# Two attention steps and an MLP: p of batches 2 to 7 turned by a DMA transpose, six output buffers, last stores on two queues, a new order of the opening

## The chip, the cores and the metric

The kernel runs on one core of a Trainium2 chip. The metric is device time in microseconds; the median of three runs before the change is 248.39 us (248.11 to 248.7). A profiled execution gives the trace that is read here.

## The reference

Shapes: 8 batches, 8 heads, 576 tokens, head size 64, 32 packed tokens; then an MLP with width 512, hidden 2048. The inputs and the output are float32.

```python
def sm_attn(qq, kk, vv):
    s = scale * np.matmul(qq, kk.transpose(0, 1, 3, 2))
    s = s - np.max(s, axis=-1, keepdims=True)
    a = np.exp(s)
    a = a / (np.sum(a, axis=-1, keepdims=True) + 1e-09)
    return np.matmul(a, vv)
p_packed = sm_attn(p, k, v)             # 32 packed tokens look at all 576
out = sm_attn(q, p_packed, p_packed)    # all 576 look at the 32
# x: out with the heads side by side, 4608 x 512
h = x @ w_in
r = np.maximum(h, 0.0)
g = s * (r * r) + b                     # s and b are scalars
return g @ w_out
```

## The kernel before, in words

Everything is computed in bf16 with float32 sums. The second attention step and the first MLP product are folded: the packed result of a batch (ppd) is multiplied with w_in once (pw, "W" below), and the hidden tile is pw times the attention weights aT, so the attention output itself is never made. The scalar s is applied and b's share added when the output leaves: ysb = s * (g part) + biasrep, where biasrep is b times the column sums of w_out.

The work of one batch, by the letters of the kernel's own list of steps:

- L: loads, all issued from the POOL queue (line 124 and after), cast from float32 on the way. k, q and v arrive with 96 rows in the partitions. Lk, Lq, Lv load a batch; Lp, Lpall load p of batch 1 and of batches 2 to 7; Lwi, Lwo load parts of w_in and w_out; Lsb loads s and b. Each of k, q and v has one buffer, so the next batch's load waits for the last reader.
- D (line 261): k and q of batches 2 to 7 are turned by a DMA transpose issued from SP, straight into kT and qT (two buffers each). T (line 222, 248): k and q of batches 0 and 1 are turned on TensorE, 12 transposes a half, and copied out of PSUM by ACT or DVE.
- V (line 268): DVE brings v into the order that the products need.
- PD, PP, PA, PPA: p is written twice side by side, turned on TensorE and copied into pbd, from which the first scores take it. Batches 0 and 1 have their own (line 186); batches 2 to 7 are one tile, pall, 96 partitions with 16 x 128 elements, turned in 16 transposes (prep_pall, line 201) and brought into pbd by eight copies, four on DVE and four on ACT.
- F, P, X, S, A: first scores and exp (line 280), product with v and division (305), its transpose into ppd (332), second scores and exp (339), and the weights by a product with ones, a logarithm, an exp of its negative and a multiplication (434). F needs kT and pbd; S needs ppd and qT.
- W (449): pw in four groups of 512 columns. M (501): a hidden tile of 128 x 576 in four matmuls of 288 columns, then relu on ACT or DVE and the square on DVE into gT. O and Q (line 545): an output tile of 128 rows in 16 matmuls of 512 columns, summed in one PSUM bank; Q evacuates it on DVE into one of five ysb buffers and stores it in two pieces (store, line 534). The last tile of all is done in two halves of 256 columns.
- BT (515): column sums of w_out on TensorE, summed and scaled on DVE. Z (596): matmuls on zeros, whose result nobody reads; they stand between real work in the first 21 us.

Batch 0 is cut into smaller steps for the opening: W0 in eight groups of 256 columns, h (line 473) in place of M, and exp0, logs0, inverse0 (lines 385 to 407) for its two parts u and, before the change, for each set a by itself.

The order is a list of words written out by hand in the kernel's last part (run, line 638). Each engine and each queue takes its own instructions in the order of this list; a helper (line 73, and lines 62 and 65 for matmul and transpose) pins it. A word with "@" names PSUM banks and issues the matmuls; the same word again, with "a" or "v", issues the evacuation on ACT or DVE. Stores and DMA transposes share SP's queue, so that an instruction that waits there holds up all behind it. On DVE, before the change, the doubling of pall (PA) stands early, in the middle of batch 1's weights; the reorder of v of batch 2 comes 15 us later.

Of the kernel before, what the change touches and what calls it, by code (L numbers as in the profile page):

```python
# [14 lines left out]
def kernel(  # L15
# [41 lines left out]
    outp = ctx.enter_context(tc.tile_pool(name="outp", bufs=5))  # L57
# [47 lines left out]
    pall = constp.tile([16 * (B - 2), 16, 2, D], BF16, name="pall")  # L105
    identb = constp.tile([P, P], BF16, name="identb")
# [24 lines left out]
    def load_part(what, part):  # L131

        if what == "q":
            if part == 0:
                raw["q", 0] = rawp.tile([R, H, NC * D], BF16, tag="qn", name="qn")
            x = slice(PARTS[part][0] * P, PARTS[part][1] * P)
            pool.dma_start(
                out=raw["q", 0][:, :, x],
                in_=q[0].rearrange("h (r c) d -> r h (c d)", c=NC)[:, :, x],
            )  # L140
            return
        if part == 0:
            raw[what, 0] = rawp.tile([R, H, NC * D], BF16, tag=what + "n", name=what + "n")
        pool.dma_start(
            out=raw[what, 0][:, 4 * part:4 * part + 4, :],
            in_={"k": k, "v": v}[what][0].rearrange("(g a) (r c) d -> a r g (c d)", a=2, c=NC)[part],
        )
# [53 lines left out]
    def prep_pall():  # L201
        n = 16 * (B - 2)
        pts = [take(1, BF16)[:, 0] for _ in range(2)]
        for t in range(16):
            tr(
                pts[t // 8][:, (t % 8) * P:(t % 8) * P + n],
                pall[:, t, :, :],
                identb[0:n, 0:n],
            )
        for x in range(2):  # L210
            yield
            src = pts[x].rearrange("p (t n) -> p t n", n=P)[:, :, 0:n].rearrange(
                "p t (x a i) -> p a x i t", a=2, i=JJ
            )
            for c2 in range(2):
                for a in range(2):
                    out = pbd[D * c2:D * c2 + D, a, 2:B, :, c2, :].rearrange(
                        "p b g (i t) -> p (b g) i t", i=JJ
                    )[:, :, :, 8 * x:8 * x + 8]
                    (act.copy if x else vec.tensor_copy)(out=out, in_=src[D * c2:D * c2 + D, a])  # L220
# [164 lines left out]
    def exp0(u, a):  # L385
        w = part(u)[1]
        act.activation(
            out=cut(e2[0][:, a], u), in_=s2[u][:, :, a * w:(a + 1) * w], func=AF.Exp, scale=scale
        )
# [7 lines left out]
    def logs0(u, a):  # L397
        w = part(u)[1]
        if ("l", u) not in rcd:
            rcd["l", u] = smp.tile([P, 2, 2 * w], F32, tag="ld", name="ld")  # L400
            rcd["r", u] = smp.tile([P, 2, 2 * w], F32, tag="rcd", name="rcd")
        act.activation(out=rcd["l", u][:, a], in_=s2["d", u][:, a, 0:2 * w], func=AF.Ln)

    def inverse0(u, a):
        act.activation(out=rcd["r", u][:, a], in_=rcd["l", u][:, a], func=AF.Exp, scale=-1.0)
# [138 lines left out]
    class Out:  # L544
        def __init__(self, col, parts, cuts=(0, NB)):
            self.col, self.parts, self.m, self.cuts = col, parts, 0, cuts
            self.yps = self.ysb = None

# [17 lines left out]
        def leave(self):  # L566
# [8 lines left out]
            for b, col, n in self.parts:  # L575
                store(self.ysb, d0, d1, i0, b, col, n, act if d0 else sp)
# [8 lines left out]
    def outs(b):  # L585
        t0, g0 = tail(b), slot(b) * S
        c0 = 0 if t0 else TAIL
        res = [Out(g0 + c0 + t * P, [(b, c0 + t * P, P)]) for t in range(NT)]
        if b % 2:
# [3 lines left out]
            res.insert(0, Out(slot(both[0][0]) * S + both[0][1], both))  # L593
# [10 lines left out]
    def ops(what, n):  # L604
# [24 lines left out]
        else:  # L629
            return {  # L630
                "h": mlp_in0, "M": mlp_in, "Z": idle, "Lpall": load_pall, "Lwo": load_w_out, "Lsb": load_sb, "PP": prep_p,
                "PA": lambda: twice(pall), "PPA": lambda _: prep_pall(), "F": first_scores, "e": exp0, "d": sums0,
# [5 lines left out]
    def run(word):  # L638
# [9 lines left out]
        elif what == "Q":  # L648
            todo[n[0], n[1]].leave()
        elif word in begun:  # L650
# [19 lines left out]
    run("Lk0.1")  # L670
    run("Lv0.0")
    run("Lv0.1")
    run("Lq0.0")
# [10 lines left out]
    run("Z12@7")  # L684

    for word in """
        Lq0.1 PD0 PP0@1 Tk0.0@2 Tk0.0a Tk0.0a PP0a Z2@0 Tk0.1@4 Tk0.1a PP0v Lp1 Tk0.1v V0.0 Z2@6 F0.0@2
        F0.0 Z5@7 P0.0@0 P0.0 F0.1@4 F0.1 Lwi0.1 Z1@1 X0.0 X0.0v V0.1 Z4@1 P0.1 P0.1 Tq0.0@2 Tq0.0a
        Tq0.0v Z2@1 Tq0.1@1 Tq0.1v Tq0.1a X0.1 X0.1v S0.0.0@6 Lwi2.4 Z1@4 S0.0.1 e0.1 S0.1.0@2 S0.1.1
        Z3@5 d0.1@0 e0.0 d0.0 e1.1 e1.0 W0.0@4 d1.1@6 l0.0 PD1 W0.0v d1.0 l1.0 i1.0 G1.0 Z6@2 W0.3@2  # L690
        W0.3v W0.3v l0.1 W0.2@0 Lwi6.8 W0.2v Z6@2 W0.7@2 l1.1 W0.6@6 i1.1 G1.1 W0.2a PP1@0 Lwi1.2 i0.1
        G0.1 W0.0a i0.0 G0.0 W0.7a PP1v PP1a W0.7a h0.6.0@4 W0.6v W0.6a W0.1@0 W0.1a W0.1a h0.6.0v
        h0.12.1@2 h0.6.0 h0.12.1a h0.12.1 h0.4.1@6 h0.14.0@4 h0.4.1a h0.14.0a h0.0.1@0 h0.0.1v h0.0.1
        h0.14.1@2 h0.14.0 h0.4.1 h0.6.1@6 h0.4.0@4 h0.6.1a h0.6.1 h0.14.1a Lk1 Tk1.0@0 h0.4.0a Tk1.0v
        Tk1.0v h0.14.1 h0.2.1@6 h0.2.1a h0.12.0@2 Lwi4.6 Tk1.1@4 Tk1.1a h0.4.0 h0.2.0@0 W0.5@6 h0.12.0a
        Tk1.1v W0.4@4 W0.4a W0.4v h0.2.0a h0.2.1 h0.12.0 W0.5v F1.0@2 F1.0 h0.0.0@4 h0.0.0v W0.5a
        h0.8.0@0 h0.8.0a F1.1@2 h0.10.0@6 Lv1 V1 h0.8.0 F1.1 P1.1@4 h0.2.0 h0.10.0a h0.0.0 h0.8.1@0
        h0.8.1a h0.10.1@2 h0.10.1a Lq1 Tq1.0@6 Tq1.0a Tq1.0a P1.1 X1 X1v Tq1.1@0 Tq1.1v W1.0@2 W1.1@4
        Tq1.1v W1.0v W1.0a S1@6,0 S1 S1 W1.3@2 W1.3v W1.3v Lwo0.4 O0.2x2@6 O0.1x2@7 Lpall O0.2x2 h0.8.1
        A1.0@0 O0.0x3@2 W1.1a W1.1a A1.0 PA O0.0x1 A1.0 A1.0 O0.3x3@3 A1.1@4 A1.1 O0.1x1 Lwo4.8 PPA0@0,1  # L700
        Lsb O0.0x1 h0.10.1 O0.0x1 O0.2x1 O0.1x1 O0.3x1 Lwo8.12 A1.1 A1.1 O0.1x2 M1.4@4 O0.3x3 Lwo12.16
        PPA0 PPA0 O0.0x2 M1.4a M1.4 h0.10.0 O0.3x1 M1.2@4 O0.1x3 M1.2a M1.2 Lv2 W1.2@0 W1.2a BT@4 Lk2
        Lq2 O0.1x1 W1.2v M1.6@0 M1.6a O0.1x1 O0.0x1 O0.1x1 Dk2 O0.3x7 M1.3@0 O0.3x1 M1.3a BT M1.5@4
        O0.2x2 M1.1@0 M1.3 M1.5a M1.5 O0.2x3 M1.6 M1.1a M1.1 M1.8@4 M1.8a O0.2x2 M1.15@0 O0.2x1 M1.15a
        V2 O0.0x2 M1.15 M1.0@4 Dq2 PPA0 Q0.3 O0.0x2 M1.0a M1.0 M1.9@0 M1.9a M1.9 M1.14@4 M1.14a O0.0x3
        Q0.0 O0.2x3 M1.7@0 Lq3 Q0.2 F2.0@4 M1.7v M1.8 F2.1@2 O0.1x1 F2.0 M1.7 O0.1x3 M1.10@0 M1.14 F2.1
        P2.1@6 Lk3 M1.10a P2.1 M1.13@4 M1.13a M1.13 M1.12@2 M1.12a X2 M1.11@0 M1.11a X2v O1.4x2@4 Q0.1
        O1.4x2 PPA0 O1.0x1@5 W2.2@2 W2.2v W2.2v S2@0,6 S2 S2 M1.11 O1.0x2 O1.4x1 O1.0x2 M1.10 A2.0@0
        A2.0 A2.0 A2.1@2 O1.1x1@6 M1.12 O1.3x2@7 W2.0@0 W2.0v W2.0v O1.0x1 Lv3 O1.1x6 W2.3@0 A2.0 Dk3
        A2.1 A2.1 A2.1 W2.1@2 W2.3a W2.3a O1.4x1 O1.3x2 Lk4 O1.3x1 O1.4x2 M2.10@0 O1.1x1 O1.3x2 M2.10v  # L710
        O1.1x1 M2.10 O1.1x2 O1.0x2 O1.1x1 M2.0@0 W2.1v W2.1a O1.0x2 O1.1x1 M2.0v M2.0 V3 M2.5@2 M2.5a
# [82 lines left out]
```

## Time and profile before

| what | us |
|---|---|
| median of three runs | 248.39 |
| the profiled execution, in all | 247.68 |
| its span, first to last instruction | 245.9 |
| TensorE matmuls busy in the span | 237.0 |
| DVE, ACT, POOL busy | 163.8, 126.9, 30.6 |
| matmuls on zeros, first 21 us | 13.5 |
| granted TensorE clock, mean | 0.997 |

The difference of 1.8 us between the execution and its span lies around the program. In the lines of the profile "L62 PE MATMUL banks<-gT" reads: line 62 of the kernel, the engine, the operation, what is written and read. PE is TensorE, PEld its weight loads, SPq, ACTq and POOLq the queues of the engines that issue DMAs. A matmul's duration contains its pipeline; the time from one start to the next is shorter. In the view of 40 slices a digit is the busy share in tenths. In the chain view the work that ended last is followed back from the end, start and length first.

### The profile page before, as it was taken

The numbers are of one execution on the slowest core, as the hardware profiler recorded it, in microseconds if no ns is written. First come the engines' busy times: TensorE is split into PE (matmuls) and PEld (weight loads), VectorE is DVE, ScalarE is ACT, GpSimd is POOL, SyncE is SP. The second block draws the span as 40 slices with busy tenths as digits, with TensorE's granted clock in tenths as the row PEclk, the third lists the DMA queues.
The fourth block names the chain that finished last, engine by engine and source line by source line (L and its number), as shares of the span: only waits on it lengthen the run. The fifth ranks groups of instructions, "written<-read, shape, count | busy, mean of one in ns | idle before, by whom it ended". The sixth has DMA issues, their size and how long they took to land.

```text
span 245.9 us, 5657 instructions
## 1 busy us (share of the span) xinstructions
PE 237.0 (96%) x2336; PEld 134.1 (55%) x2336; DVE 163.8 (67%) x330; ACT 126.9 (52%) x219; POOL 30.6 (12%) x45
## 2 busy tenths in 40 slices
PE   8998989999999999999999999999999999999991
PEld 3554765466546654665546554665456645664550
DVE  5447896998775777576678488865678756762051
ACT  2567898556745527663664437543373558830000
POOL 8743222000202010030010103001000000000000
PEclk9999999999999999999999999999999999999998
DMA  6999999999996988979976668997791112001046
GB/s 95 179 200 203 204 196 200 204 152 237 177 223 102 217 156 181 206 139 210 190 127 144 153 95 198 208 197 109 144 169 44 45 43 59 30 0 45 0 118 181
DMA packets 60522, 35.53 MB, mean 144 GB/s; under 512 B 32720, under 2 KB 56016, under 8 KB 60496
## 3 DMA queue, kind: packets, MB, share of 16 engines
q0 software_dynamic: 26272, 18.58, 52.5%
q1 hardware_dynamic: 34176, 16.55, 28.6%
q8 instruction: 18, 0.29, 0.5%
q14 instruction: 8, 0.07, 0.1%
q10 hardware_dynamic: 48, 0.03, 0.1%
HBM read 37.23 MB, written 9.44 MB: 190 GB/s over the span
## 4 chain that ended last, share of the span: by engine, by line
PE 83%; DMA 7%; DVE 3%; POOL 3%; ACT 1%; issue 1%; DVEq 0%; SPq 0%; POOLq 0%
PE banks L62 81%; DMA w_in_sb<-in_moe_w_in_dram 5%; DMA out_dram<-ysb 2%; PE banks L65 1%; DVE ysb L73 1%; POOL qn L73 1%; POOL w_in_sb L73 1%; DVE gT L73 1%; POOL kn L73 1%; POOL vn L73 1%; DVE pw L73 0%; DVE vr L73 0%; DVE rlu L73 0%; ACT rlu L73 0%; POOL pn L73 0%
## 5 line engine op out<-in xcount | busy, mean ns | idle before, releaser
L62 PE MATMUL banks<-w_out_sb,gT 128*128 128x512 bf16 (+1 forms) x592 | 144.2, 374 | 0.0
L73 ACT ACTIVATE rlu<-banks 128x576 bf16<-128x576 f32 (+2 forms) x93 | 58.2, 648 | 56.9 <-PE banks L62 41.4
L62 PEld LDWEIGHTS <-gT 128*128 128x128 bf16 x592 | 55.9, 98 | 49.5 <-issue 5.2
L62 PE MATMUL banks<-aT,pw 128*128 128x288 bf16 (+2 forms) x512 | 77.1, 286 | 0.2 <-ACT pw L73 0.2
L73 DVE TENSOR_TENSOR gT<-rlu 128x576 bf16<-128x576 bf16 (+2 forms) x128 | 54.6, 453 | 18.4 <-ACT rlu L73 17.1
L62 PEld LDWEIGHTS <-pw 128*128 128x128 bf16 x512 | 48.8, 98 | 25.0 <-ACT pw L73 0.3
L73 DVE SCALAR_TENSOR_TENSOR ysb<-banks,svec,biasrep 128x512 f32<-128x512 f32 (+1 forms) x37 | 26.6, 732 | 21.2 <-PE banks L62 17.9
L73 DVE TENSOR_SCALAR rlu<-banks 128x576 bf16<-128x576 f32 (+2 forms) x35 | 26.4, 759 | 12.2 <-PE banks L62 9.8
L73 ACT ACTIVATE e<-banks 96x768 bf16<-96x768 f32 (+3 forms) x34 | 22.2, 694 | 15.9 <-PE banks L62 12.5
L73 DVE CAST pw<-banks 128x512 bf16<-128x512 f32 (+1 forms) x34 | 20.5, 630 | 6.8 <-PE banks L62 6.7
L73 ACT CAST pw<-banks 128x512 bf16<-128x512 f32 (+1 forms) x38 | 18.7, 541 | 4.5 <-PE banks L62 4.4
L73 DVE TENSOR_TENSOR aT<-e,rcd 128x576 bf16<-128x576 bf16 (+2 forms) x18 | 11.9, 686 | 4.8 <-ACT rcd L73 4.8
L62 PE MATMUL banks<-zb 128*128 128x512 bf16 x44 | 13.5, 439 | 1.6 <-DVE zb L73 1.2
L73 POOL DMA_DIRECT2D qn<-in_q_dram x9 | 6.9, 771 | 59.0 <-DMA qT<-qn 58.6
L73 POOL DMA_DIRECT2D kn<-in_k_dram x9 | 6.9, 765 | 49.0 <-DMA kT<-kn 45.3
L73 ACT ACTIVATE ld<-banks 128x576 f32<-128x576 f32 (+2 forms) x18 | 10.6, 594 | 4.0 <-PE banks L62 3.8
L62 PE MATMUL banks<-w_in_sb,ppd 64*32 64x512 bf16 (+1 forms) x288 | 10.9, 357 | 0.6 <-DMA w_in_sb<-in_moe_w_in_dram 0.2
L73 ACT ACTIVATE rcd<-ld 128x576 f32<-128x576 f32 (+2 forms) x18 | 11.3, 631 | 0.4
L62 PEld LDWEIGHTS <-ppd 64*32 64x32 bf16 x432 | 5.1, 89 | 10.2 <-issue 6.9
L62 PEld LDWEIGHTS <-kT 128*128 128x128 bf16 x192 | 7.7, 98 | 3.3 <-issue 0.7
L73 POOL DMA_DIRECT2D vn<-in_v_dram x9 | 6.8, 752 | 16.2 <-DVE vr L73 12.8
L62 PE MATMUL banks<-pbd,kT 128*128 128x64 bf16 x192 | 8.3, 193 | 0.2 <-ACT rlu L73 0.2
(54 smaller groups left out, 95.4 us busy)
## 6 DMA issues: line engine op xcount, KB each, us to landing
out_dram<-ysb SPq DMA_DIRECT2D x23, 192.0 KB, 2.8
kn<-in_k_dram POOLq DMA_DIRECT2D x7, 576.0 KB, 9.9
vn<-in_v_dram POOLq DMA_DIRECT2D x7, 576.0 KB, 11.9
qn<-in_q_dram POOLq DMA_DIRECT2D x7, 576.0 KB, 8.2
out_dram<-ysb SPq DMA_DIRECT2D x24, 128.0 KB, 2.6
w_out_sb<-in_moe_w_out_dram POOLq DMA_DIRECT2D x4, 512.0 KB, 17.4
w_in_sb<-in_moe_w_in_dram POOLq DMA_DIRECT2D x3, 512.0 KB, 12.9
out_dram<-ysb SPq DMA_DIRECT2D x23, 64.0 KB, 2.1
```

The costliest lines, as they stand in the source:

```text
L62: return tc.keep_in_program_order(nc.tensor.matmul(*a, **kw))
L65: return tc.keep_in_program_order(nc.tensor.transpose(*a, **kw))
L73: return lambda *a, **kw: tc.keep_in_program_order(f(*a, **kw))
```

## The change

Seven things are edited.

1. pall is turned by one DMA transpose from SP (Dp) into a new tile, pallT; four copies out of SBUF (PC3, PC0, PC2 on ACT, PC1 on DVE) bring it into pbd, in place of 16 transposes and eight copies.
2. outp has six buffers and not five.
3. All output tiles of the last batch store their second piece from ACT's queue, and the first from SP's; before, this held only for the second half of the very last tile.
4. The first load of k of batch 0 (its first half) is issued as two loads of two heads.
5. exp0, logs0 and inverse0 take both sets a in one ACT instruction.
6. The order of the opening is new: eight matmuls on zeros and not twelve stand first; p of batch 1 is loaded between the halves of v; the parts of w_in come in another order; pall is loaded after the second part of w_out, s and b after k of batch 2, q of batch 3 after k of batch 4. PA stands after the reorder of v of batch 2 (V2). SP's queue now begins with p0, then pallT, kT and qT of batch 2.
7. The rest of the list has other bank numbers; in batches 6 and 7 the order of M and O tiles is another one, and the last tiles leave in the order 7.1, 7.0, 6.3, 7.3, 7.4.

```diff
-    outp = ctx.enter_context(tc.tile_pool(name="outp", bufs=5))
+    outp = ctx.enter_context(tc.tile_pool(name="outp", bufs=6))
...
+    pallT = constp.tile([P, 16, 16 * (B - 2)], BF16, name="pallT")
...
-        pool.dma_start(
-            out=raw[what, 0][:, 4 * part:4 * part + 4, :],
-            in_={"k": k, "v": v}[what][0].rearrange("(g a) (r c) d -> a r g (c d)", a=2, c=NC)[part],
-        )
+        src = {"k": k, "v": v}[what][0].rearrange("(g a) (r c) d -> a r g (c d)", a=2, c=NC)[part]
+        n = 2 if (what, part) == ("k", 0) else 4
+        for g in range(0, 4, n):
+            pool.dma_start(
+                out=raw[what, 0][:, 4 * part + g:4 * part + g + n, :], in_=src[:, g:g + n]
+            )
...
-    def prep_pall():
...
+    def turn_pall():
+        sp.dma_start_transpose(out=pallT[:], in_=pall[:].rearrange("n t c d -> n (t c d)"))
+
+    def prep_pall(a, c2, on):
+        x = slice(D * c2, D * c2 + D)
+        to(
+            on,
+            pbd[x, a, 2:B, :, c2, :].rearrange("p b g (i t) -> p (b g) i t", i=JJ),
+            pallT[x].rearrange("p t (x a i) -> p a x i t", a=2, i=JJ)[:, a],
+        )
...
-    def exp0(u, a):
+    def exp0(u):
         w = part(u)[1]
         act.activation(
-            out=cut(e2[0][:, a], u), in_=s2[u][:, :, a * w:(a + 1) * w], func=AF.Exp, scale=scale
+            out=e2[0][:].rearrange("p a (i s) -> p i a s", i=2)[:, :, :, part(u)[0]],
+            in_=s2[u][:, :, 0:2 * w].rearrange("p i (a s) -> p i a s", a=2),
+            func=AF.Exp,
+            scale=scale,
         )
...
-                store(self.ysb, d0, d1, i0, b, col, n, act if d0 else sp)
+                store(self.ysb, d0, d1, i0, b, col, n, self.other)
...
-        t0, g0 = tail(b), slot(b) * S
+        t0, g0, other = tail(b), slot(b) * S, act if b == B - 1 else sp
...
-    run("Z12@7")
+    run("Z8@7")
...
-        h0.8.1a h0.10.1@2 h0.10.1a Lq1 Tq1.0@6 Tq1.0a Tq1.0a P1.1 X1 X1v Tq1.1@0 Tq1.1v W1.0@2 W1.1@4
-        Tq1.1v W1.0v W1.0a S1@6,0 S1 S1 W1.3@2 W1.3v W1.3v Lwo0.4 O0.2x2@6 O0.1x2@7 Lpall O0.2x2 h0.8.1
...
+        Lwo0.4 P1.1@2 P1.1 Tq1.0@4 X1 Tq1.0v Tq1.0a Tq1.1@6 X1v W1.3@2 Tq1.1v W1.1@4 h0.10.1a Tq1.1v
+        W1.3v W1.3a S1@0,6 S1 S1 O0.1x3@2 O0.2x1@3 W1.1v W1.1v A1.0@0 A1.0 O0.2x2 A1.1@6 A1.1 h0.12.1
...
+        O0.0x1 M1.6 M1.5@0 M1.5a O0.3x2 O0.1x3 Lq2 M1.10@0 M1.7 O0.1x1 BT O0.1x3 M1.10a Dp PC3a PC0a
+        O0.2x2 PC2a O0.3x2 O1.4x1@7 O0.1x2 O0.2x1 O0.1x1 O1.4x1 O0.2x1 M1.5 O1.4x3 Dk2 Dq2 Q0.0 PC1v
+        F2.0@0 F2.0 Q0.3 F2.1@4 F2.1 Q0.1 Q0.2 O1.4x1 M1.15 O1.4x2 M1.10 M1.11@2 Lk3 P2.1@6 P2.1 M1.11a
```

## The prediction, made before the changed kernel had run

> **What bounds the kernel now.** First the page: engine shares, slices, chain.
>
> ```profile
> span 245.9 us, 5657 instructions
> PE 237.0 (96%) x2336; PEld 134.1 (55%) x2336; DVE 163.8 (67%) x330; ACT 126.9 (52%) x219; POOL 30.6 (12%) x45
> ...
> PEclk9999999999999999999999999999999999999998
> DMA  6999999999996988979976668997791112001046
> ...
> PE 83%; DMA 7%; DVE 3%; POOL 3%; ACT 1%; issue 1%; DVEq 0%; SPq 0%; POOLq 0%
> ```
>
> TensorE is busy 96% and carries 83% of the chain; DMA is full only in the first quarter. So I asked where TensorE waits at all: the timeline of TensorE around 34 to 41 us (start, length, then the group).
>
> ```profile
> 34.04 0.67 PE L65 MATMUL banks<-identb,qn 96*128 96x96 bf16 x12
> ...
> 35.51 0.63 PE L62 MATMUL banks<-w_in_sb,ppd 64*32 64x512 bf16 x16
> 35.95 0.77 PE L62 MATMUL banks<-qT,ppd 64*32 64x288 bf16 x16
> 36.90 0.41 PE L62 MATMUL banks<-w_in_sb,ppd 64*32 64x512 bf16 x8 [0.18 <-DVE pw L73]
> 37.34 1.46 PE L62 MATMUL banks<-w_out_sb,gT 128*128 128x512 bf16 x6
> ...
> 40.85 0.84 PE L65 MATMUL banks<-identb,pall 96*128 96x96 bf16 x16
> 41.53 1.68 PE L62 MATMUL banks<-w_out_sb,gT 128*128 128x512 bf16 x7
> ```
>
> From 37.34 the start-to-start times are constant: 216 ns for a 512-column matmul, 122 ns for 288. The last one ends at 240.41 (240.13 + 0.28). So whatever leaves that row, or makes it begin earlier, is gained whole; whatever puts a hole into it is lost whole. Before 37.34 the pace is that of the loads (k of batch 0 lands at 5.50 and 7.17, the four w_in parts at 16.25 to 22.43, k1 25.29, the last w_in 27.82, v1 30.80, q1 33.67, the first w_out 36.33: each one's issue plus landing time), and 44 filler matmuls take 13.5 us of it.
>
> Last, the end: the chain and the timeline of the final stretch.
>
> ```profile
> 235.59 0.66 DVE ysb L73
> 236.25 0.00 issue
> 236.25 0.75 DVE ysb L73
> 237.00 0.45 SPq L73
> 237.45 0.05 issue
> 237.50 2.47 DMA out_dram<-ysb
> 239.98 0.03 issue
> 240.00 0.05 DVEq L73
> 240.05 0.04 issue
> 240.10 0.75 DVE ysb L73
> ```
> ```profile
> 233.38 9.53 SPq L73 DMA_DIRECT2D out_dram<-ysb  x15
> ...
> 240.10 1.14 DVE L73 SCALAR_TENSOR_TENSOR ysb<-banks,svec,biasrep 128x512 f32<-128x512 f32 x2 [0.63 <-DMA out_dram<-ysb]
> 241.27 0.37 ACTq L73 DMA_DIRECT2D out_dram<-ysb  x1
> ```
>
> TensorE is done at 240.41, but VectorE stands at 240.10 because all five output buffers are still being stored. The last output is ready at 241.24; SP, 0.3 to 0.6 us a store and 15 of them in a row, issues its last at 242.53. That lands at 244.92 (2.39 later), and the span closes 0.98 after: a tail of 5.49 us behind TensorE.
>
> **The turn of p, on TensorE.** Removed: 16 transposes of pall, 40.85 to 41.53: **0.68 us** of the gap-free row. Also removed: eight copies out of PSUM (four on DVE at 0.55, four on ACT at 0.47), which lay beside it.
>
> **The turn of p, elsewhere.** Added: one DMA transpose, pall to pallT, first in SP's queue, and four SBUF copies of 64x768 (three ACT, one DVE). Neither is in the trace. The nearest row for the transpose is kT<-kn: 24 blocks, issue 3.0, landing 5.1. pallT has 16: issue 2.0, landing 2.0+2.1 = 4.1. The Trainium skill (DMA: Bandwidth & Descriptors, "Latency and other measured facts" and "Anatomy of one DMA") states 261 GB/s for such a transpose and 2 us fixed: 393 KB gives 3.5, an estimate. I keep the row's 4.1; range 3.5 to 6. For a copy: ACT, 0.47 at 384 elements, with about 0.22 fixed, gives 0.72 at 768; rlu at 768 takes 0.81. I take 0.8, range 0.5 to 1.1. On DVE 0.45 (twice as fast as the PSUM row) to 0.9.
>
> Does it stay hidden? In the new order F2.0, the first scores of batch 2, needs pallT, its copies, and kT of batch 2, whose own transpose now waits behind pallT on SP; qT's and all stores are behind that. Walk:
> - The DVE copy that doubles pall now stands behind the reorder of v2. v2 landed at 49.56; DVE gets there at about 49.4 (its queue follows TensorE). Reorder 0.95, one product 0.45, doubling 0.42: 51.4.
> - pallT issues at 51.4, lands at 55.5; kT issues at 53.4, lands at 58.5; qT issues at 56.4, lands about 61.2.
> - ACT, after the rlu of M1.10 (56.75), makes its three copies: the one F2.0 needs by 58.4, the last by 59.2. DVE, after the doubling: two products, the bias sums (0.68+3x0.72+4x0.49 = 4.8), a product, an output row: 58.0; its copy 58.5 to 58.9.
> - TensorE reaches F2.0 after 69 matmuls of 512 (14.9), 12 M tiles (5.9), two pairs of sums, two W1, bias sums (2.2) from the first output matmul at 36.75 (below): 59.7.
> So the slack is 0.8 to 1.2 us, and the cost **zero**; without that cover it is microsecond for microsecond. S2 needs qT at about 64: slack over 2. POOL: k3 waits for kT's landing 0.8 later than before, but q3 now goes after k4, so k3 is issued earlier than its 61.70 of before.
>
> **The opening.** Loads: same bytes, one issue more (0.7), pn moved up. POOL's issues run up to 20 us ahead of landings, so k1, v1, q1 and w_out keep their times. Removed: four filler matmuls ahead of the first k (cold, 0.43 each), a half-size first load, and half of the ACT calls of exp, Ln and inverse (12 become 6). All this is before the loads' pace: it costs or gains only by what is still open when q1 lands. ACT and DVE were busy 10.8 and 10.7 of the 12 us from 22 to 34, so they set how late q1's transposes begin (34.04, 0.37 behind the landing). Now the h tiles start at about 21.1, not 21.55 (the w_in part they need comes first, at 16.7; ten fillers of 0.22 and W0.7, W0.6 follow W0.3 from 17.7 on), so I let q1's turn begin at 33.75: 0.51 of transposes, X1 0.11, the second 0.51, two qT copies on DVE to 36.1, S1 0.6: output matmuls from **36.75**, not 37.34: -0.59. But one W1 group of eight (0.35) that lay ahead of them lies behind now: +0.35. Net **-0.24**, bounds -1.0 and +1.0.
> A rule speaks against dropping fillers: TensorE: Matmul & The Clock Gate, "The HAM clock gate", says full clock comes only after some 3.4 us of sustained work, on a free-running window. The trace has full clock from 5.65, 4.5 after the first filler; eight fillers end at 4.6, then there is little until k lands at about 5.5. By the rule's worst case the window is missed, and 12+12 transposes at half clock cost 24 x 0.04 = 1 us there; the row (a 16 us stretch of waits and fillers follows) absorbs it. I take 0.
>
> **The tail.** Six buffers remove the wait of 0.63 at 240.10. The last batch's second parts go to ACT: of the last two tiles SP issues two stores, ACT two. The new order puts about 2.2 us of matmuls between the third-last tile and the next, so DVE is idle when TensorE ends: last evacuation 0.47, stores at T+0.55; ACT's landed 2.75 after issue: T+3.3; close 0.98: a tail of 4.3, **-1.2** (bounds -0.6, -1.5). The Trainium skill ("Issuing engines are not separate DMA queues", same DMA page) says a second issuing engine saves only sequencer issue time, usually small: by that rule 0 here, were SP not behind. The row shows it 1.3 behind (242.53 against 241.24), so I take the row.
>
> **Sum.** -0.68 - 0.24 - 1.2 = -2.1: span 245.9 to 243.8. That execution took 247.68 in all; the median of three is 248.39, so I subtract from the median: **246.3 us**.
>
> **Rivals.**
> - F2.0 late but mild: pallT or kT takes 1 to 3 us longer than its row (transposes of batches 3 and 4 took up to 5.9). For it: q2 loads at the same time, DMA full. Hole 0.3 to 2.5: 246.6 to 248.8.
> - *Slower*: the same chain with v2 late. One mechanism: SP's head waits for DVE, which waits for v2, so pallT, kT and F2.0 slide together. It decides when kT lands later than 59.7+2.6 = 62.3, 3.8 later than worked out: over 248.9. Against it: v2 has svec and bvec (1.5 us of the queue) no longer ahead of it.
> - The opening late: cold clock and three kT copies on DVE leave ACT's evacuations behind, so output matmuls begin at 38 to 39: 247.5 to 248.6. Against: pacing by loads.
> - The tail doesn't move: the last landing is bound by the DMA, not SP: 247.5.
>
> **How the numbers follow.** As worked out: 0.62 (own range 245.3 to 247.2). Tail unmoved 0.06. F2.0 mild 0.16, half of it within 0.2% (247.9 to 248.9, about what a measurement of this kernel tells from no change), half faster. Opening late 0.08: 0.03 faster, 0.04 same, 0.01 slower. Slower rival 0.08. Faster 0.62+0.06+0.08+0.03 = 0.79; same 0.12; slower 0.09. Range: down to 245.2 (opening and tail at their better bounds, half each), up to 248.3, which leaves out the slower rival and the upper ends of the others.
>
> **What would show it.** No hole in TensorE between 37 us and its end, which comes near 239.5; first output matmul near 36.8; kT of batch 2 landed before 59; no DVE wait for a store at the end and a tail near 4.3. Wrong if TensorE has a hole of over 1 us before the first scores of batch 2, or output matmuls begin after 38.

## The result, and the profile after

The changed kernel takes **254.22 us** (median of four, 252.89 to 254.53), the kernel before 248.25 beside it: a ratio of 1.0232, 95% interval 1.021 to 1.0254. It is 2.3% slower; 246.3 was predicted. The profiled execution took 254.53, its span 252.8. The kernel before took 247.3 to 250.5 in 108 of 109 executions (one took 252.0), but some variants below spread from 247 to 255 with no gap between, so ranges stand beside the medians.

The page of the changed kernel:

```profile
span 252.8 us, 5587 instructions
PE 236.0 (93%) x2285; PEld 133.8 (53%) x2319; DVE 164.9 (65%) x329; ACT 125.9 (50%) x210; POOL 32.8 (13%) x46
...
PEclk9999999999999999999997999999999999999999
...
PE 73%; DMA 15%; DVE 3%; issue 2%; ACT 2%; POOL 2%; SPq 0%; POOLq 0%; DVEq 0%
```

DMA's share of the chain has doubled, from 7% to 15%, and the clock row has a 7 just past the middle. TensorE's timeline in the changed kernel, at the places that matter:

```profile
38.13 1.02 PE L62 MATMUL banks<-w_out_sb,gT 128*128 128x512 bf16 x3 [0.18 <-DVE pw L73]
...
61.62 0.51 PE L62 MATMUL banks<-pbd,kT 128*128 128x64 bf16 x12 [0.32 <-ACT pbd L73]
63.04 0.51 PE L62 MATMUL banks<-pbd,kT 128*128 128x64 bf16 x12 [0.90 <-ACT pbd L73]
...
131.73 3.66 PE L62 MATMUL banks<-w_out_sb,gT 128*128 128x512 bf16 x10 [3.63 <-DVE ysb L73]
```

And two stretches around the last of these (start and end, length, then busy time and number of instructions of PE, PEld, DVE, ACT and POOL, the granted clock, DMA's share, GB/s):

```profile
127.70:131.70 4.00, 0.39 (x9) 0.11 (x2) 2.31 (x4) 2.32 (x5) 0.00 (x0) 1.00 1.05 178
...
132.50:136.00 3.50, 3.50 (x12) 1.42 (x10) 1.61 (x3) 0.00 (x0) 0.59 (x1) 0.51 0.57 63
```

TensorE's row ends at 248.77 and not at 240.41. From start to start, where a hole is 0.16 longer than the idle time in the brackets, the 8.36 us are: first output matmul 38.13 and not 37.34, +0.79; the W1 group that moved behind it, +0.35; the 16 transposes gone, -0.68; holes at the two first scores of batch 2, 0.48 + 1.07; a hole of 0.85 near 94; a hole of 3.80 at 127.7; and 1.7 for the 3.41 us at half clock behind it. The tail behind TensorE is 3.98 and not 5.49: -1.5. So the tail did what was said, and a wait 64 us behind the last instruction that the prediction walked through cost most. The chain of the changed kernel (start, length, what) leads there:

```profile
88.73 5.50 DMA qT<-qn
...
106.03 6.09 DMA kT<-kn
...
114.23 15.14 DMA vn<-in_v_dram
...
130.27 0.75 DVE aT L73
131.01 0.67 DVE ysb L73
131.73 5.69 PE banks L62 x23
```

VectorE stood 5.68 us before the reorder of v5, which landed at 129.37 (119.63 before). Its timeline there:

```profile
129.39 0.95 DVE L73 COPY vr<-vn 96x3072 bf16<-96x3072 bf16 x1 [5.68 <-DMA vn<-in_v_dram]
```

An output's evacuation was queued behind it, and TensorE waited for that PSUM bank. Here kT4 is the turned k of batch 4, and q4 the load of q of batch 4. v5 is late because k5 is, k5 because kT4, that because q4 is, and q4 because it waits for qT3. First the kernel before, its loads on POOL (start, issue time, wait ahead of it):

```profile
77.36 0.77 POOL L73 DMA_DIRECT2D kn<-in_k_dram  x1 [13.98 <-DMA kT<-kn]
...
89.77 0.77 POOL L73 DMA_DIRECT2D qn<-in_q_dram  x1 [10.88 <-DMA qT<-qn]
```

And its transposes on SP (start, issue time):

```profile
71.70 3.19 SPq L73 DMA_TRANSPOSE kT<-kn  x1
...
83.40 3.82 SPq L73 DMA_TRANSPOSE qT<-qn  x1
```

The loads of the changed kernel on POOL:

```profile
78.59 0.78 POOL L73 DMA_DIRECT2D kn<-in_k_dram  x1 [15.92 <-issue]
79.36 0.77 POOL L73 DMA_DIRECT2D qn<-in_q_dram  x1
...
96.36 0.77 POOL L73 DMA_DIRECT2D qn<-in_q_dram  x1 [15.47 <-DMA qT<-qn]
```

And its transposes on SP:

```profile
69.56 5.77 SPq L73 DMA_TRANSPOSE kT<-kn  x1
...
88.73 3.53 SPq L73 DMA_TRANSPOSE qT<-qn  x1
...
121.28 6.88 SPq L73 DMA_TRANSPOSE kT<-kn  x1
```

kT3's issue takes 5.77 and not 3.19, beside v3's load (it lands 7.85 later and not 5.06). q3, behind k4, lands at 88.60, and qT3, which had gone out at 83.40, starts there. That is 6.6 at q4 (96.36 against 89.77). kT5 then starts with q5 and v5 still coming (6.88; 3.53 before, when v5 was nearly in), and v5 takes 15.1 us from its issue and not 12.0.

### The profile page after: what moved, and what is told of

It reads as the page before. It is cut to its first block, busy times and chain, and to the rows that moved or that the text cites. A ratio compares the mean times of both kernels' runs of the same rounds, so it can differ in the third digit from the quotient of the medians.

```text
span 252.8 us, 5587 instructions
## 1 busy us (share of the span) xinstructions
PE 236.0 (93%) x2285; PEld 133.8 (53%) x2319; DVE 164.9 (65%) x329; ACT 125.9 (50%) x210; POOL 32.8 (13%) x46
## 3 DMA queue, kind: packets, MB, share of 16 engines
HBM read 37.23 MB, written 9.44 MB: 185 GB/s over the span
## 4 chain that ended last, share of the span: by engine, by line
PE 73%; DMA 15%; DVE 3%; issue 2%; ACT 2%; POOL 2%; SPq 0%; POOLq 0%; DVEq 0%
PE banks L62 72%; DMA vn<-in_v_dram 6%; DMA pallT<-pall 2%; DMA kT<-kn 2%; DMA qT<-qn 2%; DMA pn<-in_p_dram 2%; ACT pbd L73 2%; PE banks L65 1%; POOL kn L73 1%; POOL identb L73 1%; DVE qT L73 1%; DVE kT L73 0%; DVE ysb L73 0%; SPq L73 0%; ACT rlu L73 0%
## 5 line engine op out<-in xcount | busy, mean ns | idle before, releaser
L62 PE MATMUL banks<-w_out_sb,gT 128*128 128x512 bf16 (+1 forms) x561 | 140.2, 376 | 6.1 <-DVE ysb L73 3.6
L73 ACT ACTIVATE rlu<-banks 128x576 bf16<-128x576 f32 (+2 forms) x87 | 55.1, 654 | 59.6 <-PE banks L62 41.8
L62 PE MATMUL banks<-aT,pw 128*128 128x288 bf16 (+2 forms) x512 | 77.9, 287 | 0.3
L73 DVE TENSOR_TENSOR gT<-rlu 128x576 bf16<-128x576 bf16 (+2 forms) x128 | 55.2, 455 | 17.4 <-ACT rlu L73 15.8
L73 DVE TENSOR_SCALAR rlu<-banks 128x576 bf16<-128x576 f32 (+2 forms) x41 | 30.7, 750 | 13.5 <-PE banks L62 8.3
L73 ACT CAST pw<-banks 128x512 bf16<-128x512 f32 (+1 forms) x44 | 21.0, 541 | 4.3 <-PE banks L62 4.3
L73 DVE CAST pw<-banks 128x512 bf16<-128x512 f32 (+1 forms) x28 | 17.2, 638 | 2.0 <-PE banks L62 1.8
L73 POOL DMA_DIRECT2D kn<-in_k_dram x10 | 7.6, 756 | 68.8 <-DMA kT<-kn 52.0
L62 PE MATMUL banks<-zb 128*128 128x512 bf16 x40 | 12.5, 436 | 1.3 <-DVE zb L73 1.2
L73 DVE COPY vr<-vn 96x3072 bf16<-96x3072 bf16 (+1 forms) x9 | 8.2, 913 | 7.7 <-DMA vn<-in_v_dram 7.7
```

What stands on the lines that cost most here:

```text
L62: return tc.keep_in_program_order(nc.tensor.matmul(*a, **kw))
L73: return lambda *a, **kw: tc.keep_in_program_order(f(*a, **kw))
```

## Experiments

**1. q3's place, and the first load.** First theory: q3 behind k4 makes the loss; for the opening, the split first load. Four variants of the changed kernel.

q3 early:

```diff
-        M1.11@2 Lk3 P2.1@6
+        M1.11@2 Lk3 Lq3 P2.1@6
...
-        W2.3a Lq3 M2.0@4
+        W2.3a M2.0@4
```

> Kernel after, with one step moved: the load of q of batch 3 goes back ahead of v3 and k4 in POOL's queue (right behind k3). Theory (the load order makes the loss): q3 is issued near 63.1 when qT2 has landed, not at 79.36; q4, k5, q5 and v5 follow some 7 us earlier, v5 lands before 123, TensorE's hole of 3.81 at 127.7 and the 3.41 us at half clock behind it (1.7 lost) are gone: 254.2 - 5.5 = 248.7 (range 248.2 to 249.5). Rival (the DMA turn of p makes it: SP's queue is late by pallT, and everything behind it stays late): q3, now in front, only waits for qT2 and holds k4 up; v5 is still late, 252 to 254.5.

Measured 253.05 (252.49 to 254.54), ratio 1.0191 (1.0147 to 1.0234): 1.2 gained, not 5.5. q3 is issued at 63.25, but kT3's transpose now lies beside q3's and v3's loads (6.03), qT3's beside k4's and v4's (7.50); q4 is issued at 97.13, as late as in the changed kernel; v5 lands at 129.56, with a hole of 3.06 at 128.6. The theory falls.

The memset first:

```diff
+    vec.memset(pbd[:, :, 1:B], 0.0)
     vec.memset(pbd[:, :, 0], 0.0)
...
-    vec.memset(pbd[:, :, 1:B], 0.0)
```

> Kernel after, with one VectorE instruction moved: the big memset of pbd (128x1792, 1.55 us) stands ahead of the small ones and not behind, so that it ends near 2.76, when POOL's affine_select of identb begins; the split first load is kept. Theory (the two instructions were in each other's way: affine_select took 1.87 us, from 2.76 to 0.28 behind the memset's end): affine_select takes 0.3 to 0.4, the third load of k0 is issued near 3.1 and not at 4.59, all loads up to w_out land 1.3 to 1.5 earlier, output matmuls begin near 37.2 and not 38.13: 253.3 (252.9 to 253.7), the later hole untouched. Rival (the longer time belongs to the extra issue ahead of it, or to POOL alone): affine_select still takes over 1.5, loads and start unmoved, 254.2.

Measured 252.77 (249.34 to 253.91). The collision is as said. POOL's timeline in the changed kernel:

```profile
2.76 1.87 POOL L73 TENSOR_SCALAR_AFFINE_SELECT identb<-identb 128x128 bf16<-128x128 bf16 x1
```

VectorE's timeline in the changed kernel:

```profile
2.80 1.55 DVE L73 MEMSET pbd<- 128x1792 uint32 x1 [0.32 <-issue]
```

POOL's timeline with the memset first:

```profile
2.77 0.30 POOL L73 TENSOR_SCALAR_AFFINE_SELECT identb<-identb 128x128 bf16<-128x128 bf16 x1
```

POOL's timeline in the kernel before:

```profile
2.17 0.30 POOL L73 TENSOR_SCALAR_AFFINE_SELECT identb<-identb 128x128 bf16<-128x128 bf16 x1
```

The extra issue moved affine_select by 0.6 us into the memset; it ended 0.28 behind the memset's end (4.63 against 4.35). The Trainium skill (SBUF — State Buffer, "SBUF: two separate sides") has the rule that VectorE and GpSimd share one pair of ports, which one of them holds for a whole instruction while the other waits. The rows agree that one waited until the other was done, but not on which: the page gives the pair to the one that starts first, and affine_select, which waited, starts 0.04 before the memset by the record. The page names VectorE operations in a two-port mode or with two inputs there, and not memsets.

For the start this bought less than expected: the loads just behind it are issued 1.6 earlier and most land only 0.3 to 0.9 earlier (q1 at 34.69 and not 34.99), and the first output matmul stayed at 38.13.

The first load whole:

```diff
-        n = 2 if (what, part) == ("k", 0) else 4
+        n = 4
```

> Kernel after, with one part undone: the first half of k of batch 0 is one load again and not two. Theory: affine_select is back at 2.17 with 0.30, out of the memset's way; the second half of k0 is issued at 2.4, 2.2 earlier; loads land at least as early as in the run with the memset moved (one issue of 0.7 less), output matmuls begin at 37.0 to 37.3: 253.2 (252.7 to 253.7). Rival (the early quarter of k0 is worth more than the late rest costs): the first transposes begin 0.3 to 0.5 later, clock comes later, no gain: 254.0 to 254.6.

Measured 252.56 (249.65 to 253.37); q1 landed at 33.81, first output matmul at 36.90; in later variants with the whole load 36.55, 36.98, 37.13, 37.87 and 39.08. In the eight traces with the split it is 37.55 to 38.82, the memset moved or not. So the split costs about 1 us between the medians (37.06 and 38.13), and the 36.75 of the prediction is near the best that the new opening gives without it. The kernel before is no firmer: six traces with its opening begin at 37.34 to 39.79, and the one read for the prediction was the earliest. The +0.79 between two single executions is therefore not shown to be the change's. The late holes stay (2.96 at 125.9), with q3 at 86.34 and qT3 at 93.71.

q3 early and the memset first, both edits:

> Kernel after, with q3's load moved back and the memset first, both edits together. Theory (two separate causes): the gains add, -5.5 and -0.9: 247.8 (247.3 to 248.7), faster than the kernel before only by what the tail gives, because the two holes at the first scores of batch 2 (1.55) stay. Rival (one cause only, the late opening pushes all later loads into each other): no better than the better of the two alone, within 0.3.

Measured 252.91 (252.82 to 253.23): no sum of gains; a hole of 2.5 stays at 129.0.

**2. The loads' loop.** Second theory: loads wait for transposes, transposes run slower beside loads, so lateness feeds itself. The changed kernel with q3 first (order q3, k3, v3, as in the kernel before):

```diff
-        M1.11@2 Lk3 P2.1@6
+        M1.11@2 Lq3 Lk3 P2.1@6
...
-        W2.3a Lq3 M2.0@4
+        W2.3a M2.0@4
```

> Kernel after, with q3's load one place further ahead than in the first run of this kind: q3, k3, v3 as in the kernel before (there it stood k3, q3, v3). Theory (a DMA transpose that runs beside loads takes twice as long, and the loads wait for transposes in turn): kT3's transpose runs beside v3's load alone, is issued in 3 to 4 us and not 6.0, qT3's in about 4 and not 7.5; v5 lands before 124, no hole at 128: 248.5 (247.8 to 249.5). Rival (the place of q3 does nothing; TensorE's two holes at the first scores of batch 2, and so SP's stores, make all that follows late): v5 lands at 128 to 130 again, 252.5 to 253.5.

Measured 254.83 (253.77 to 255.1), ratio 1.0264: the rival's line, though above its range. kT3 takes 2.95 again, but k3 lands at 75.33 only; q4 at 97.02.

The kernel before with q3 late:

```diff
-        M1.7@0 Lq3 Q0.2
+        M1.7@0 Q0.2
...
-        O1.3x2 Lk4 O1.3x1
+        O1.3x2 Lk4 Lq3 O1.3x1
```

> Kernel before, with this one part of the change: the load of q of batch 3 is issued behind k4's. Nothing else differs. Theory (the order of the loads makes the loss): q3 is issued near 78 and not at 60.9, qT3 lands near 95 and not at 89.2, v5 near 126 and not at 119.6; VectorE waits for it, TensorE stands 2 to 4 us near 126, with 1.7 more at half clock: 251.5 to 254. Rival (the loss needs the late start and the holes at batch 2 as well): under 249.2.

Measured 248.67 (median of 18), ratio 1.0019 (0.9995 to 1.0043): the same. q3's place costs the kernel before nothing that these executions (247.44 to 252.09) show. q3 is issued at 76.02, but qT3 lands at 90.93, 1.7 later than before, and v5 (121.44) is still in time. The kernel before with q3 in the middle:

```diff
-        M1.7@0 Lq3 Q0.2
+        M1.7@0 Q0.2
...
-        P2.1@6 Lk3 M1.10a
+        P2.1@6 Lk3 Lq3 M1.10a
```

> Kernel before, with q3 and k3 exchanged in POOL's queue: k3, q3, v3. Theory (transposes beside loads): kT3's transpose is issued 3 to 4 us earlier than at 71.7, but beside q3's and v3's loads; its issue takes about 6 and not 3.2, and k4 and v4 then lie beside qT3's transpose (7 and not 3.8 us); v5 lands at 123 to 127, a hole of 0 to 3 us near 126: 248.5 to 252. Rival (only the long delay of q3 behind k4 counts): within 0.3 of before.

Measured 248.69, ratio 1.0012 (0.9991 to 1.0032). kT3 takes 6.40 and k4 is 2.3 late; v5 at 122.42, no hole. A transpose beside loads is slow, but that alone doesn't run away.

The changed kernel with v5's reorder later:

```diff
-        W4.3v Lk6 V5 Dk6
+        W4.3v Lk6 Dk6
...
-        W4.2a Q3.1 M4.3@2
+        W4.2a Q3.1 V5 M4.3@2
```

> Kernel after, with one VectorE instruction moved: the reorder of v of batch 5 stands some 9 us later in VectorE's order, behind the outputs 3.0 and 3.1, still ahead of the product that reads it at 148.5. All loads and transposes keep their places. Theory (this wait of 5.68 us on v5, with the outputs behind it, is what stops TensorE): no hole at 127.7, no half clock, 254.2 - 5.5 = 248.7 (248.2 to 249.5), with v5 still landing near 129. Rival (the late transposes stop TensorE elsewhere as well: the first scores of batch 5 wait for kT5, landing near 132): a hole of 2 to 4 us there, 250.5 to 253.

Measured 252.59 (249.38 to 253.59); the profiled execution 251.81. The wait did what was said: from F4.0 to F5.1 19.41 us and not 24.89, so hole and half clock cost 5.48. But the late loads found the next wait. VectorE's timeline with v5's reorder moved:

```profile
171.33 0.96 DVE L73 COPY vr<-vn 96x3072 bf16<-96x3072 bf16 x1 [2.79 <-DMA vn<-in_v_dram]
```

TensorE's timeline there:

```profile
173.00 0.65 PE L62 MATMUL banks<-aT,pw 128*128 128x288 bf16 x4 [2.37 <-DVE rlu L73]
```

v6, behind q7, and q7 behind qT6: the lateness is the loads' own and moves on.

**3. Where it begins: the transpose of p in SP's queue.** Third theory: pallT, ahead of kT2 and qT2, makes both 2 to 3 us late, and the loop does the rest. The changed kernel with the first load whole and p early:

```diff
-        M1.14 PA O0.0x2
...
-        M1.10a Dp PC3a PC0a O0.2x2 PC2a O0.3x2
...
-        Dk2 Dq2 Q0.0 PC1v
+        M1.4@0 M1.4v PA Dp O0.2x1
...
+        M1.7a PC0a V2 O0.0x2
...
+        M1.15a PC2a O0.2x3
...
+        M1.7 PC1v O0.1x1 BT
...
+        M1.10a PC3a O0.2x2 O0.3x2
```

> Kernel after with the first k load whole, and p of batches 2 to 7 turned earlier: the doubling of pall stands ahead of the reorder of v2 (near 44), the transpose goes out right behind it, and the four copies are spread over 50 to 59 on ScalarE and VectorE. q3's load stays behind k4. Theory (pallT ahead of kT2 in SP's queue, and the copies behind it, are the first lateness, and the rest grows from it): kT2 is issued near 52 and lands near 57, no hole at the first scores of batch 2 (1.1 gained), v5 lands before 123, no hole near 126: 246.5 (245.5 to 248). Rival (q3 behind k4 is what makes the transpose of q3 late once TensorE is early): the hole of 1.1 goes, v5 still lands at 125 to 127, a hole of 2 to 4 near 126 stays: 250.5 to 252.5.

And with q3 first as well, as in part 2:

> The same, and q3's load ahead of k3 as in the kernel before; so all three suspects are undone or moved away (first load, place of pallT, place of q3), and the transpose of p by DMA, six buffers and the stores on two queues are kept. Theory (any of these): the loads and transposes of batches 3 to 5 run as in the kernel before, q4 issued near 90, v5 landed near 120, no hole from 37 to the end, tail of 4: 245.3 (244.8 to 246.5). Rival (the loads' own contention with stores and transposes is set off by TensorE being early, whatever the order): v5 lands after 124, 248.5 to 252.

Measured 254.26 and 253.96: both wrong, for a reason of their own. ScalarE's timeline with p early and q3 first:

```profile
58.08 1.48 ACT L73 COPY pbd<-pallT 64x768 bf16<-64x768 bf16 x1 [6.77 <-DMA pallT<-pall]
```

TensorE's timeline there:

```profile
60.16 1.12 PE L62 MATMUL banks<-aT,pw 128*128 128x288 bf16 x4 [5.80 <-ACT rlu L73]
```

pallT, issued at 44.46 among the opening's loads, lands at 58.06, 13.6 later, and the copies put early stop ScalarE for 6.77. The two say nothing on the theory; they say that a transpose issued there is had no earlier (58.06, against 58.48 in the changed kernel, where it is issued at 52.34).

The changed kernel with the first load whole and q3 first, p where the change has it:

> Kernel after with the first k load whole and q3's load ahead of k3; pallT stays where it is, ahead of kT2 and behind the doubling near 50.7. Theory (pallT ahead of kT2 is the first lateness): kT2 lands near 58.1, qT2 near 61, q3 is issued near 61.6, k3 lands near 74, kT3 near 79, qT3 beside k4 and v4; v5 lands at 126 to 128, a hole of 3 to 4 near 127: 251.5 to 254. Rival (late start plus q3's place, both now undone): 246.5 to 248.

Measured 252.75 (250.88 to 253.31): qT2 at 61.98, q3's load takes 8.9 us (7.0 before), k3 lands at 74.36, kT3 at 79.76, q4 at 96.25; holes of 1.4 at 78.2 and 2.6 at 127.8. As the theory has it.

The kernel before with one transpose more:

```diff
+    spare = constp.tile([P, 16, R], BF16, name="spare")
...
+    def turn_more(b):
+        sp.dma_start_transpose(
+            out=spare[:], in_=raw["k", b][:].rearrange("r h x -> r (h x)")[:, 0:16 * P]
+        )
...
-        O0.1x1 Dk2 O0.3x7
+        O0.1x1 Dz2 Dk2 O0.3x7
```

> Kernel before, with one DMA transpose added ahead of kT2 on SP: 16 blocks of 96x128 of k2's raw tile into a spare tile that nobody reads, the size of pallT. Nothing else differs. Theory (a transpose more ahead of kT2 sets off the growth): kT2 lands 2 to 2.8 later than at 57.7, the first scores of batch 2 wait about 1.5, q3 is issued 2 to 3 later, and the lateness grows to 5 or more at v5 (lands after 125): 251.5 to 254. Rival (kernel before has the slack, lateness does not grow): 248.4 + 1 to 2 = 249.4 to 250.4, v5 lands by 123.

Executions of 250.66, 252.22, 255.05 and 255.33, ratio of the shorter two 1.0119 (1.0053 to 1.0184). kT2 lands at 59.90, 2.2 late; q3's load takes 9.6, kT3 lands at 82.73, 6.0 late. TensorE's timeline there:

```profile
82.78 0.82 PE L62 MATMUL banks<-pbd,kT 128*128 128x64 bf16 x12 [3.40 <-DMA kT<-kn]
```

2.2 us at kT2 have become 6 one batch later, and the hole is there and not at v5, which lands at 123.82. One transpose on SP, with no work for any engine, costs the kernel before 2 to 7 us.

**4. The turn alone, without, and the tail alone.**

The kernel before with the turn by DMA (pallT, turn_pall and prep_pall as in the change), all PPA words gone:

```diff
-        A1.0 PA O0.0x1
+        A1.0 PA Dp O0.0x1
...
-        M1.14@4 M1.14a O0.0x3
+        M1.14@4 M1.14a PC0a PC2a O0.0x3
...
-        Q0.0 O0.2x3
+        Q0.0 PC1v PC3v O0.2x3
```

> Kernel before with the turn of p by DMA alone: 16 transposes and eight copies out, one DMA transpose behind the doubling of pall (issued near 42) and four copies in, two on ScalarE and two on VectorE, just ahead of the first scores of batch 2. Theory (the transpose, among the last opening loads, makes k2, kT2 and qT2 late, and the lateness grows): pallT lands at 55 to 58, kT2 near 60, qT2 near 62.5, first scores of batch 2 late by 1 to 2, kT3 after 80, holes of 2 to 5 in all: 250.5 to 254. Rival (the turn itself is harmless; the changed opening is what hurts): -0.7 from the transposes, +0 to 0.7 at the first scores: 247.6 to 248.4.

Measured 253.21 (252.54 to 255.22), ratio **1.0218** (1.0183 to 1.0254): the turn alone does to the kernel before what the whole change did. pallT takes 13.4 us from issue to landing, kT2 lands at 59.24, q4 is issued at 96.21, v5 lands at 127.68; holes at the first scores, of 1.6 near 93 and of 2.0 at 127.8. SP's timeline there:

```profile
39.37 4.16 SPq L73 DMA_TRANSPOSE pallT<-pall  x1
54.02 3.13 SPq L73 DMA_TRANSPOSE kT<-kn  x1
```

The path is not the third theory's: pallT had landed (52.74) before kT2 went out, and SP's queue held nothing up. kT2 waited for k2's load, beside which pallT moved: it landed at 53.94, in the five other traces with this opening at 51.8 to 53.2. That pallT slowed it is argued from these rows. Either way kT2 is late, by 1.5 here and by 2.8 in the changed kernel.

The changed kernel with the turn left out:

```diff
-                "PA": lambda: twice(pall), "Dp": turn_pall,
+                "PA": lambda: (vec.memset(pallT[:], 0.5), None)[1], "Dp": turn_pall,
...
-        M1.10a Dp PC3a PC0a
+        M1.10a PC3a PC0a
```

> Kernel after with the DMA turn of p left out: no transpose of pall is issued, the doubling is replaced by filling pallT with a constant (so p of batches 2 to 7 is not used; the four copies, all loads and all orders stay). Theory (the turn makes the lateness): kT2 is issued when k2 lands (52.7), lands near 57.8, qT2 near 60.5; k3 is issued near 58.4, v5 lands before 123; the hole at 127.7 and the half clock are gone, the hole of 1.1 between the two first scores of batch 2 stays, because the copies stay: 247.7 (247.2 to 248.8). Rival (the new order of the loads and opening makes it): v5 still at 126 to 130, 251.5 to 254.

Of twelve executions five took 247.7 to 249.5, seven 252.1 to 255.4 (median 252.27). The profiled one, 247.95, is as the theory says: kT2 at 57.48, q4 at 91.22, v5 at 119.92, no hole but 0.76 between the first scores. So without the turn the new order can keep pace, and often doesn't. All four executions of the changed kernel were over 252; against twelve that are mixed, four are too few to say how much the turn adds there.

The same with the first load whole and q3 first:

> The same (the DMA turn of p left out, pallT filled with a constant), with the first k load whole and q3's load ahead of k3. Theory (the turn alone is at fault): output matmuls from 36.9, no hole but the 1.1 between the first scores of batch 2, tail 4: 246.6 (246.0 to 247.3). Rival (early TensorE sets off the contention by itself): v5 after 124, 249 to 252.

Twenty executions, spread from 247.3 to 254.9 (median 251.13); the theory's 246.6 came in none. The profiled one, 254.16, has late loads (q4 at 96.68, v5 at 128.94, hole 2.8), so the turn isn't the only way in.

The kernel before with points 2 and 3 of the change, nothing else:

```diff
-    outp = ctx.enter_context(tc.tile_pool(name="outp", bufs=5))
+    outp = ctx.enter_context(tc.tile_pool(name="outp", bufs=6))
...
-                store(self.ysb, d0, d1, i0, b, col, n, act if d0 else sp)
+                store(self.ysb, d0, d1, i0, b, col, n, self.other)
```

> Kernel before with the tail part of the change alone: six output buffers, and the second pieces of the last batch's stores from ScalarE's queue; orders untouched. Theory (the tail gain of 1.5 us in the changed kernel comes from these two): VectorE does not wait for a store at 240.1, SP's last store is issued near 241.8, tail of 4.3 to 4.6 and not 5.49: 248.3 - 1.0 = 247.3 (247.0 to 247.6). Rival (it comes from the new order of the last tiles): tail 5.2 or more, 248.0 to 248.4.

Measured **247.30** (246.95 to 247.61), ratio 0.9953 (0.9939 to 0.9968): tail 4.43 and not 5.50. The other 0.45 to 3.98 is left for the order of the last tiles, which wasn't tried alone. Buffers and queues weren't tried apart.

**5. Keep the turn, move the waits.**

The reorder of v4 goes behind X3a, v5's as in part 2, v6's load ahead of q7's; in the first of two runs the first load is whole too, and the copies of p are split two and two:

```diff
-        P3.1@4 V4 O1.4x1
+        P3.1@4 O1.4x1
...
-        O2.0x4 X3a S3@4,6
+        O2.0x4 X3a V4 S3@4,6
...
-        F5.0@2 F5.0 Lq7
+        F5.0@2 F5.0 Lv6 Lq7
...
-        M5.1@0 Lv6 M5.8@2
+        M5.1@0 M5.8@2
...
-        M1.10a Dp PC3a PC0a
+        M1.10a Dp PC0a
...
-        Q0.0 PC1v
+        Q0.0 PC1v PC3v
```

> Kernel after with the DMA turn of p kept, and what waits moved out of TensorE's way: the first k load whole; two of the four copies of p on VectorE (ahead of output 0.3) and two on ScalarE; the reorder of v4 behind the turn of batch 3's packed product, the reorder of v5 behind output 3.1, v6's load ahead of q7's. Theory (the loads of batches 3 to 5 stay late, but TensorE does not depend on them so early): v5 lands at 125 to 128 as in the run with the first load whole, no hole over 0.5 us from 37 to the end, tail 4: 246.0 (245.2 to 247.0), faster than the kernel before. Rival (the lateness shows at the next wait: first scores of batch 4 or 5 for kT4 or kT5, second scores of batch 3 for qT3): one hole of 1.5 to 4, 248.5 to 251.5.

Measured **246.52** (246.09 to 247.44 in six executions; one of 619.65 stands apart, was not traced and stays unexplained), ratio **0.9937** (0.9914 to 0.996): 0.6% faster than the kernel before. The tail alone gave 0.9953, and the two intervals overlap, so a gain from the turn itself is not shown. Its page:

```profile
span 244.3 us, 5585 instructions
...
PE 233.8 (96%) x2285; PEld 133.1 (54%) x2319; DVE 165.4 (68%) x330; ACT 124.3 (51%) x209; POOL 30.8 (13%) x45
```

TensorE's timeline there, its one wait of over 0.2 us behind 37:

```profile
93.18 0.44 PE L62 MATMUL banks<-qT,ppd 64*32 64x288 bf16 x16 [0.50 <-DMA qT<-qn]
```

The loads are still late (q4 93.72, v5 124.14), but no engine asks for them so early.

Only the three waits moved, first load and copies as in the change:

> Kernel after with only the three waits moved (reorders of v4 and v5 later on VectorE, v6's load ahead of q7's); first load split as in the change, three copies of p on ScalarE. Theory (the waits cost most, the first load and the copies the rest): no hole at 127 nor at 170, no half clock behind them; 254.2 - 5.5 - 0.5 = 248.2 (247.6 to 249.2), some 1.7 above the run with all repairs (start 1.2 to 1.5 later, hole of 1.1 between the first scores of batch 2). Rival (the late start brings another wait of the late loads to the front: qT3 for the second scores of batch 3, kT5 for the first scores of batch 5): 249.5 to 252.

Measured 248.10 (247.55 to 249.8), ratio 0.9989 (0.9969 to 1.0009), with q4 at 95.69 and v5 at 127.29. So moving the three waits is worth some 6.1, all that the change had lost; a whole first load and divided copies are worth another 1.3 (by the ratios) to 1.6 (by the medians).

In one table (us; the first three columns from the profiled executions, the time the median where nothing else is said):

| kernel | kT2 landed | q4 issued | v5 landed | time |
|---|---|---|---|---|
| before | 57.73 | 89.77 | 119.63 | 248.25 |
| before, tail alone | 56.91 | 89.83 | 119.79 | 247.30 |
| before, q3 late | 57.81 | 91.48 | 121.44 | 248.67 |
| before, q3 in the middle | 58.55 | 92.15 | 122.42 | 248.69 |
| changed, turn left out | 57.48 | 91.22 | 119.92 | 247.95 (this one) |
| before, one transpose more | 59.90 | 95.89 | 123.82 | 255.05 (this one) |
| before, turn alone | 59.24 | 96.21 | 127.68 | 253.21 |
| changed | 60.51 | 96.36 | 129.37 | 254.22 |
| changed, q3 early / first | 59.78 / 59.90 | 97.13 / 97.02 | 129.56 / 129.96 | 253.05 / 254.83 |
| changed, three waits moved | 59.70 | 95.69 | 127.29 | 248.10 |
| all repairs | 58.09 | 93.72 | 124.14 | 246.52 |

In all twenty traces q4 is issued by 92.2 or not before 93.7. That sorts the traces; the times of one variant show no such gap. In the last two rows q4 is late, and little or nothing is lost.

## Why the prediction was wrong

**The step that failed** is the walk's last: "So the slack is 0.8 to 1.2 us, and the cost zero; without that cover it is microsecond for microsecond." The slack was negative, the cost is not proportional, and the loads behind kT2 and qT2 were put at nothing. Both of its own signs of being wrong came, a start behind 38 and a hole of over 1 us. Against its own profiled execution the forecast was 247.68 - 2.1 = 245.6, and 254.53 came: 8.9 more. Of it 1.4 is the start (38.13, not 36.75), 1.55 the two holes at the first scores, 6.3 what came behind them, less 0.3 from the tail. The holes are the copies, ScalarE's timeline:

```profile
58.51 4.48 ACT L73 COPY pbd<-pallT 64x768 bf16<-64x768 bf16 x3 [0.40 <-DMA pallT<-pall]
```

They took 1.49 each (taken 0.8, range to 1.1; VectorE's 0.85 was in its range), behind a pallT of 6.14 (taken 4.1, range to 6). The 3.5 worked out from the Trainium skill (DMA: Bandwidth & Descriptors, "Latency and other measured facts" and "Anatomy of one DMA") was further off still; the same sum gives 4.3 for the 24 blocks of kT, an estimate, and 4.3 to 5.1 was measured with few or no loads beside them. So it fits a transpose by itself, and leaves out the loads beside it. The second of the three copies was ready at 61.5 and the last at 63.0, not 59.2. kT2, at 60.51 and not 58.5, was in time for TensorE.

The 6.3 came where the walk had stopped. It followed k3 ("issued earlier than its 61.70": it was, 61.11) and didn't ask further who waits for kT2 and qT2: q3, k3, then kT3 and qT3, k4 and q4, with transposes that take longer beside loads (kT3's issue 5.77, beside v3's load, and not 3.19). 2.8 us at kT2, against the kernel before, became 6.6 at q4 and 9.7 at v5.

**The slower rival** had the mechanism ("pallT, kT and F2.0 slide together") and a wrong point: it "decides when kT lands later than 59.7+2.6 = 62.3". With kT at 60.51 the time was already over its 248.9, because the point was worked out from the direct hole alone. Its cause, v2 late, wasn't it either: v2 landed at 49.80, 0.2 late.

**The transposes on TensorE, -0.68**: they are gone from the row; it holds as a term, hidden by the rest.

**The opening, -0.24**: the term "one issue more (0.7) ... keep their times" failed. The third load of k was issued 2.2 later than the second had been (4.59 against 2.41), 1.6 of it from the collision, and q1 landed 1.3 later. How much of the 1.4 this made is open, because q1 lands anywhere from 33.67 to 35.35 in the six traces with the opening of the kernel before. As to the clock rule weighed there (the Trainium skill, TensorE: Matmul & The Clock Gate, "The HAM clock gate"), the clock was full from 6.25 in this execution, and from 3.84 to 7.07 in the twenty traces, which agrees with a window of some 3.4 us that does not begin with the kernel. Two traces then fell back to half clock for one window: one with the opening of the kernel before, twelve fillers ahead of the first k (q3 in the middle, from 9.44 to 12.86, a start at 39.79), one with the new opening, eight fillers (the turn left out and the load whole, from 8.83 to 12.24, a start at 39.08). A start at 39.03 came without it. So the four fillers less are not shown to matter, and "I take 0" stands.

**The tail, -1.2**: right, and a little small: -1.5, of it 1.07 from buffers and queues. The Trainium skill (DMA: Bandwidth & Descriptors, "Issuing engines are not separate DMA queues") allows a second issuing engine just the time to issue. Taken as 0, that would have missed what the rows show: SP's last store was issued 2.13 behind TensorE's end in the kernel before, and 0.74 in the run with the tail alone. Of that 0.32 is the last output being ready sooner (0.52 behind TensorE's end and not 0.84).

What is shown: the turn by itself is enough to make the loss (part 4), so is an empty transpose ahead of kT2 (part 3), and early waits turn the lateness into time on TensorE (part 5). Leaving the turn out of the changed kernel doesn't mend it reliably, seven of twelve executions were late all the same, so the new order of opening, loads and stores has a part of its own. What stays open is which. In the late trace without the turn q3's load took 9.3 and not 7.0, while eight stores left SP from 61.2 on; but the kernel before issues as many from 58.8 on, beside a q3 load of 7.0, so the stores by themselves don't explain it.

## What to carry to other kernels

An operation that is hidden from the engine that bounds the kernel can still set back a loop of transfers that wait for each other. Follow its delay through the loop until a wait absorbs it, with the durations that transfers have beside each other and not alone, and look at each engine's order for a wait on late data with other work queued behind it. A wait that stands earlier than its result is needed costs nothing until the data is late: moving three such waits was worth more (6.1 us) than all that the change set out to gain.

## What was not expected of the hardware

- A DMA transpose of the same 24 blocks was issued in 2.4 to 3.2 us and landed in 4.3 to 5.1 with the DMA engines to itself or nearly; beside loads, in up to 7.6 and 11.1. Of 16 blocks, 4.5 to 6.1 beside q2's load, and 13.4 to 13.7 among the opening's loads.
- TensorE's clock changes only on a raster of 3.41 us: in all twenty traces the stretches between its changes are whole multiples of it. Behind the opening, full clock gave way to half where one step of the raster held 2.09 us or more without a matmul (2.09 to 2.65 in seven traces, the whole step in two), and not where the emptiest held 1.83 or less. So a hole of 2.55 brought a step at half clock (2.38 of it lay in one step), and one of 3.06 none (1.79 and 1.09 in two). The price of 1.7 more is a matter of where a hole falls.
- An SBUF to SBUF copy of 64x768 bf16, read with a stride, took 1.49 on ScalarE (1.9 ns an element) and 0.85 on VectorE; ScalarE's relu out of PSUM takes 0.65 for 576.
